# Two-level attention and a ReLU-squared layer: scores centred on the mean of h, softmax without transposes, four square blocks per 960 tokens

## The chip, the cores and the metric

One core of one Trainium2 chip runs the whole program. The metric is the device time in microseconds of one execution, the median of several. Engines: TensorE (PE in the profile, its weight loads PEld), VectorE (DVE), ScalarE (ACT), GpSimd (POOL); SyncE (SP) issues the DMAs.

## The reference

```python
x: [4, 12480, 128], inducing: [32, 128]; w_in: [128, 2048], w_out: [2048, 128]
def mab(q, kv):
    s = q @ kv.T / sqrt(128); a = softmax(s)       # over kv's rows
    return a @ kv
h = mab(inducing, x)            # per batch, 32 rows
y = mab(x, h)                   # per batch, 12480 rows
out = relu(y @ w_in) ** 2 @ w_out
```

Each row of y is a mean of 32 rows of h with weights a near 1/32. A hidden column keeps one sign for all tokens unless it is "mixed"; over the columns of positive sign the layer is a quadratic form in a, and both kernels compute it as such: products of differences a_i - a_j, squared, times 128-wide matrices made from w_in, h and w_out. Mixed columns are computed one by one.

## The kernel before, in words

x comes in twice: transposed (`xT`, fp32, tokens along the free axis) and in natural order (`xn`). A batch has 26 chunks of 480 tokens in 7 groups G of four (the last of two).

- `first(b)`: per group, scores of the inducing rows (line 226, four column groups of TensorE), evacuation with the scale and running maxima (245, `sT`); then the global maximum (260 to 271, `nb`), exp on ACT (286), four transposes (297, `et`) evacuated to `en`, products with `xn` (310, `hacc`) added up in `hq` (318). `largest` (277) takes abs-maxima of x on DVE, for a bound. At the end h and its transpose `hT` (327 to 333).
- `prepare(b)`: columns w_in against h (398, `hwv`), per-column signs (`pos`, `dead`, `mix`) from bounds, a linear part (482, `R`), a selection of up to 64 mixed columns (`hot`, 505 to 546), and four matrices of pair products (554, `G`; 558, `wq`) scaled into `w16` (559).
- `second(b, G)`: scores of x against h (226), evacuation (`s2`), transposes (350, `s2t`), token-major softmax (353 to 364: maximum, subtraction, exp, sum, reciprocal, product), transposes back (368, `at`), split into two fp16 halves (370, 371), stored to DRAM (`ad`, 372) and loaded again as `aT` with the 32 weights on each row quarter (382).
- `Chunk`: `up` multiplies `aT` by fixed difference matrices `pairs` (two tiles of two banks, each from two products on 64 rows, 591) and by `singles` (one bank of its own); `lift` squares the two wide tiles on ACT (603), and clips `singles` on DVE (607, `tmp`) and squares it on POOL (608); `down` sums a linear product (613, `lin`) and five products with `w16` (616) in one bank `po`, which ACT or DVE evacuates with scale and bias (620, 622), followed by the store of `o` (623).

Before the main loop come batch 0's `first`, the conversion of the weights from float64 words (`narrow`, 196 to 202), w_out's maximum (`prepare_w_out`, 208 to 213) and `prepare(0)`. In the main loop, chunk n's lifts, chunk n+1's ups and chunk n-1's downs are issued in turns, and `background(k)` hands out steps of `second` and of the next batch's `first` and `prepare` by fixed rates per chunk. Within what the buffers and data allow, a list scheduler with costs of its own orders each engine's queue; `to_act` chooses ACT or DVE for an evacuation by sums of estimated costs (`held`). A last part, entered only if a batch's flag says that the bounds fail (`flags`), computes all 2048 columns.

Of the kernel before, what the change touches and what calls it, by code (L numbers as in the profile page):

```python
# [9 lines left out]
F32 = mybir.dt.float32  # L10
# [27 lines left out]
def attend_then_relu2_mlp(ctx: ExitStack, tc: tile.TileContext, xn, xT, indT, w_in, w_out, outT):  # L38

# [20 lines left out]
    ps_s = ctx.enter_context(tc.tile_pool(name="ps_s", bufs=1, space=bass.MemoryType.PSUM))  # L60
# [14 lines left out]
    nc.vector.tensor_copy(rep, fold[:, 0:1].broadcast_to([P, 4, MI]))  # L75
    ones = const.tile([1, P], F32, name="ones")
# [15 lines left out]
    cut4 = const.tile([P, 1], F32, name="cut4")
    nc.vector.memset(cut4[0:64], 0.0)
    nc.vector.memset(cut4[64:P], -3e38)

    pairs = const.tile([P, 2 * P], F16, name="pairs")
    fold_f = fold.rearrange("p k i -> p (k i)")
    for s in range(1, 17):
        c, m = (s - 1) // 4, (s - 1) % 4
        rows = slice(64 * (c % 2), 64 * (c % 2) + 64)  # L100
        nc.vector.tensor_tensor(
            pairs[rows, P * (c // 2) + MI * m:P * (c // 2) + MI * (m + 1)], fold_f[rows, 0:MI], fold_f[rows, s:s + MI],
            op=ALU.subtract,
        )
# [4 lines left out]
    inv_t = const.tile([P, 1], F32, name="inv_t")  # L109
    flags = const.tile([1, NB], F32, name="flags")  # L110
# [5 lines left out]
    for k in range(2):  # L116
        one = Batch()
        one.xm = const.tile([P, NG], F32, name=f"xm{k}")
        one.hn = const.tile([P, P], F32, name=f"hn{k}")
        one.w16 = const.tile([P, NQ, P], F16, name=f"w16_{k}")  # L120
        one.lin = const.tile([P, P], F16, name=f"lin{k}")
        one.singles = const.tile([P, P], F16, name=f"singles{k}")
        nc.vector.memset(one.w16, 0.0)
        nc.vector.memset(one.singles, 0.0)
        nc.vector.tensor_copy(one.singles[0:64, 64:96], fold[0:64, 0])
        one.osc = const.tile([P, 1], F32, name=f"osc{k}")
        one.bias = const.tile([P, 1], F32, name=f"bias{k}")
# [21 lines left out]
    def evac(dst, src, cols, by=None):  # L149

        if to_act(120 + 0.833 * cols, 110 + 1.042 * cols):
# [19 lines left out]

# [34 lines left out]
    def prepare_w_out():  # L206
# [5 lines left out]
        nc.vector.reciprocal(t, inv_t)  # L212
        nc.scalar.mul(w_hi, wo_sb, t)
        yield


    def load_xT(b, G, again=False):
        pool, bufs = (mlp, 2) if again else (flow, NX)
        xp = pool.tile([P, 4, 4, TP], F32, tag="xp", name=f"xp_{b}_{G}_{again}", bufs=bufs)
        n = GRP[G]  # L220
        nc.sync.dma_start(xp[:, 0:n], xT[:, b, 16 * G:16 * G + 4 * n, :].rearrange("c (n q) p -> c n q p", q=4))
        return xp

    def scores(ps, lhsT, xp, n):
        for q in range(4):
            nc.tensor.matmul(  # L226
                ps[32 * q:32 * q + 32, 0:n * TP].rearrange("i (n p) -> i n p", p=TP),
                lhsT, xp[:, 0:n, q, :], start=True, stop=True,
            )

    def first(b):

        st = sts[b]
        sT = flow.tile([P, NCH * TP], F32, tag="sT", name=f"sT_{b}", bufs=1)
        mx = work.tile([P, NG], F32, tag="mx", name=f"mx_{b}")
        for G, n in enumerate(GRP):
            if b:
                st.xp[G] = load_xT(b, G)
                yield
            ps = att_psum(f"s1_{b}_{G}")  # L240
            xg = st.xp[G]
            scores(ps, indT_sb, xg, n)
            w = n * TP
            held["dve"] += 150 + 1.042 * w
            nc.vector.tensor_scalar(
                sT[:, 480 * G:480 * G + w], ps[:, 0:w], scale, None, op0=ALU.mult, op1=ALU.max, accum_out=mx[:, G:G + 1],
# [3 lines left out]
        def load_xn(h):  # L250

            if h >= NCH // 2:
                return None
            t = xnb[h % XB]
            nc.sync.dma_start(t, xn[b].rearrange("(p k) c -> p k c", p=TP)[:, 8 * h:8 * h + 8, :])
            return t

        xns = {h: load_xn(h) for h in range(XB)}
        m1 = small("m1")
        nc.vector.tensor_reduce(m1, mx, axis=AX.X, op=ALU.max)  # L260
# [13 lines left out]
        def largest(G):  # L274
            n = GRP[G]
            held["dve"] += 60 + 1.042 * 4 * n * TP
            nc.vector.tensor_reduce(  # L277
                st.xm[:, G:G + 1], st.xp[G][:, 0:n].rearrange("p n q t -> p (n q t)"), axis=AX.X, op=ALU.max,
                apply_absolute_value=True,
            )  # L280

        def exp(G):
            n = GRP[G]
            s = sT[:, 480 * G:480 * G + n * TP]
            held["act"] += 200 + 0.833 * n * TP
            nc.scalar.activation(s, s, AF.Exp, bias=nb, accum_out=zs[:, G:G + 1])  # L286

        zs = work.tile([P, NG], F32, tag="zs", name=f"zs_{b}")
        exp(0)
        exp(1)  # L290
        yield
        hq = work.tile([P, P + 1], F32, tag="hq", name=f"hq_{b}", bufs=1)
        for G, n in enumerate(GRP):
            ps = att_psum(f"et_{b}_{G}") if b else two_banks(f"et_{b}_{G}")[:, 0]
            for j in range(n):
                c = 4 * G + j
                nc.tensor.transpose(ps[0:TP, j * P:(j + 1) * P], sT[:, c * TP:(c + 1) * TP], ident)
            en = work.tile([TP, 4, P], F32, tag="en", name=f"en_{b}_{G}")
            evac(en[:, 0:n], ps[0:TP, 0:n * P].rearrange("p (n m) -> p n m", m=P), n * P)
            if G + 2 < NG:  # L300
                exp(G + 2)
            largest(G)
            yield
            hacc = att_psum(f"hacc_{b}_{G}")
            for h in range(n // 2):
                xg = xns.pop(2 * G + h)
                for j in (2 * h, 2 * h + 1):
                    c = 4 * G + j
                    for q in range(4):
                        st.last = nc.tensor.matmul(  # L310
                            hacc[32 * q:32 * q + 32, 0:P], en[:, j, 32 * q:32 * q + 32],
                            xg[:, 4 * (j % 2) + q, :], start=j == 0, stop=j == n - 1,
                        )
                xns[2 * G + h + XB] = load_xn(2 * G + h + XB)
# [4 lines left out]
            if G == NG - 1:  # L319
                nc.vector.tensor_reduce(hq[:, P:P + 1], zs, axis=AX.X, op=ALU.add)  # L320
            yield
        hs = att_psum(f"hs_{b}")
        nc.tensor.matmul(hs[:, 0:P + 1], rep.rearrange("p q i -> p (q i)"), hq, start=True, stop=True)
# [8 lines left out]
        nc.vector.tensor_reduce(st.hT[:, P:P + 1], ht[:, 0:MI], axis=AX.X, op=ALU.add)  # L332
        nc.vector.tensor_scalar(st.hT[:, P:P + 1], st.hT[:, P:P + 1], 1.0 / MI, None, op0=ALU.mult)
        yield

    def second(b, G, again=False):

        st = sts[b]
        n = GRP[G]
        t = 4 * n  # L340
        w = n * TP
        xp = st.xp.pop(G)
        ps = att_psum(f"s2_{b}_{G}")
        scores(ps, st.hT[:, 0:MI], xp, n)
        s2 = work.tile([P, 480], F32, tag="s2", name=f"s2s_{b}_{G}")
        evac(s2[:, 0:w], ps[:, 0:w], w)
        yield
        pt = att_psum(f"s2t_{b}_{G}")
        for j in range(n):
            nc.tensor.transpose(pt[0:TP, j * P:(j + 1) * P], s2[:, j * TP:(j + 1) * TP], ident)  # L350
        pv = pt[0:TP, 0:n * P].rearrange("p (t i) -> p t i", i=MI)
        mx = work.tile([TP, 16], F32, tag="mx2", name=f"mx2_{b}_{G}")
        nc.vector.tensor_reduce(mx[:, 0:t], pv, axis=AX.X, op=ALU.max)  # L353
        e = work.tile([TP, 16, MI], F32, tag="e2", name=f"e2_{b}_{G}")
# [536 lines left out]
```

## Time and profile before

| | |
|---|---|
| runs | 592.66 us median of 3 (591.72, 592.66, 596.0) |
| profiled execution | span 594.4 us, first to last instruction; it lies inside the range of the runs |
| busy: PE, PEld, DVE, ACT, POOL | 475.1, 229.3, 412.2, 326.5, 107.2 us |
| mean granted TensorE clock | 0.901 |
| DMA | 100.89 MB, 56.3% of 16 engines' time |
| first evacuation of an output tile | 132.11 us |
| last evacuation | 584.95 us |

A group's row reads: line, engine, operation, out<-in with shapes, count, busy time and mean ns of one, then the idle time just before it and what ended most of it. A row of the timeline starts with its start and its length in us; x8 stands for eight instructions in a row. An fp32 product is two records.

### The profile page before, as it was taken

What the parts mean: (1) busy time and instruction counts of PE and PEld (TensorE: products, weight loads), DVE (VectorE), ACT (ScalarE), POOL (GpSimd) and SP (SyncE); (2) the same over time, 40 slices, a digit from 0 to 9 for tenths busy, and PEclk for the clock granted to TensorE, in tenths of its full rate; (3) what the DMA queues carried; (4) which work ended last, traced back from release to release, by engine and by line L of the source; (5) the groups of instructions that cost most, each with busy time, mean ns of one, the idle gap of its engine ahead of it and who ended that gap; (6) DMA issues with size and microseconds to landing.
All of it is one profiled execution on the core that took longest, in us unless ns stands there. A gap on an engine that the chain in (4) does not pass through costs nothing. (4 is left out here: it accounts for less than half of the span.)

```text
span 594.4 us, 9822 instructions
## 1 busy us (share of the span) xinstructions
PE 475.1 (80%) x3539; PEld 229.3 (39%) x3539; DVE 412.2 (69%) x979; ACT 326.5 (55%) x475; POOL 107.2 (18%) x113
## 2 busy tenths in 40 slices
PE   4261373879899699988999799889998999899992
PEld 0140251643244265532344346433453455333330
DVE  6999519677774338877862578888844587888761
ACT  0040101247598346656698476475796565767770
POOL 0000000022031012112222111122211121233340
PEclk9775555899999759989999799999999899999998
DMA  8989473104669954346579863547588213254522
GB/s 343 327 212 243 160 193 115 52 1 156 211 191 239 267 149 145 109 157 220 145 211 259 247 189 117 183 133 215 167 223 224 79 51 101 83 178 139 167 108 79
DMA packets 52671, 100.89 MB, mean 170 GB/s; under 512 B 8476, under 2 KB 42268, under 8 KB 52604
## 3 DMA queue, kind: packets, MB, share of 16 engines
q1 hardware_dynamic: 52604, 100.08, 56.3%
q8 instruction: 32, 0.52, 0.4%
q14 instruction: 35, 0.29, 0.2%
HBM read 68.11 MB, written 31.95 MB: 168 GB/s over the span
## 5 line engine op out<-in xcount | busy, mean ns | idle before, releaser
L603 ACT ACTIVATE g<-hp 128x960 f16<-128x960 f32 x208 | 194.7, 976 | 43.3 <-PE hp L591 41.9
L608 POOL TENSOR_TENSOR g<-tmp 128x480 f16<-128x480 f32 x104 | 106.0, 1019 | 471.6 <-DVE tmp L607 271.0
L616 PE MATMUL po<-g,w 128*128 128x480 f16 x520 | 139.5, 378 | 0.4 <-ACT w L155 0.3
L607 DVE TENSOR_SCALAR tmp<-hs,off,cut 128x480 f32<-128x480 f32 x104 | 80.1, 770 | 28.8 <-PE hs L591 24.4
L591 PE MATMUL hp<-aT,pairs 64*128 64x480 f16 x416 | 87.6, 375 | 7.6 <-ACT g L603 7.5
L616 PEld LDWEIGHTS <-w 128*128 128x128 f16 x520 | 49.1, 99 | 71.1 <-issue 37.2
L620 ACT ACTIVATE o<-po,bias,osc 128x480 f32<-128x480 f32 x72 | 54.8, 761 | 33.8 <-PE po L616 28.5
L277 DVE TENSOR_REDUCE xm<-xp_False 128x1 f32<-128x1920 f32 (+1 forms) x28 | 56.0, 2002 | 7.0 <-DMA xp_False<-xT_dram 7.0
L613 PE MATMUL po<-aT,lin 128*128 128x480 f16 x104 | 39.8, 382 | 17.0 <-ACT o L620 12.0
L591 PEld LDWEIGHTS <-pairs 64*128 64x128 f16 x416 | 22.6, 93 | 75.0 <-issue 73.9
L310 PE MATMUL hacc<-xnb,en 120*32 120x128 f32 x832 | 36.0, 307 | 13.5 <-DMA xnb<-xn_dram 6.7
L591 PE MATMUL hs<-aT,singles 128*128 128x480 f16 x104 | 38.9, 374 | 2.6 <-DVE tmp L607 2.0
L226 PE MATMUL s<-xp_False,indT_sb 128*32 128x480 f32 (+1 forms) x224 | 29.8, 610 | 12.2 <-DMA xp_False<-xT_dram 8.3
L310 PEld LDWEIGHTS hacc<-xnb,en 120*32 120x32 f32 x832 | 23.3, 121 | 28.6 <-issue 9.8
L554 DVE TENSOR_TENSOR G<-hwp,hw 128x512 f16<-128x512 f16 x64 | 27.4, 459 | 8.1 <-PE wq L558 8.1
L286 ACT ACTIVATE sT<-sT,nb 128x480 f32<-128x480 f32 (+1 forms) x28 | 18.5, 665 | 26.5 <-DVE nb L271 26.5
L622 DVE TENSOR_SCALAR o<-po,osc,bias 128x480 f32<-128x480 f32 x32 | 24.8, 774 | 11.8 <-PE po L616 11.4
L226 PE MATMUL s<-xp_False,hT 128*32 128x480 f32 (+1 forms) x224 | 29.1, 593 | 1.2 <-DVE a L371 1.0
L359 ACT ACTIVATE e<-e 120x512 f32<-120x512 f32 (+1 forms) x28 | 16.9, 602 | 24.0 <-DVE e L355 23.7
L318 DVE TENSOR_TENSOR hq<-hacc,hq 128x128 f32<-128x128 f32 x24 | 6.9, 288 | 32.0 <-PE hacc L310 32.0
L153 ACT COPY en<-et 120x512 f32<-120x512 f32 (+1 forms) x26 | 14.4, 554 | 25.3 <-PE hacc L310 15.3
L353 DVE TENSOR_REDUCE mx<-s2t 120x16 f32<-120x512 f32 (+1 forms) x28 | 18.2, 649 | 10.5 <-PE s2t L350 9.9
(209 smaller groups left out, 586.9 us busy)
## 6 DMA issues: line engine op xcount, KB each, us to landing
xnb<-xn_dram SPq DMA_DIRECT2D x52, 480.0 KB, 6.4
outT_dram<-o SPq DMA_DIRECT2D x104, 240.0 KB, 2.5
xp_False<-xT_dram SPq DMA_DIRECT2D x24, 960.0 KB, 5.9
aT<-ad SPq DMA_DIRECT2D x96, 120.0 KB, 4.4
ad<-a SPq DMA_DIRECT2D x24, 240.0 KB, 2.4
wi<-w_in_dram SPq DMA_DIRECT2D x4, 512.0 KB, 15.7
wo<-w_out_dram SPq DMA_DIRECT2D x4, 512.0 KB, 7.0
xp_False<-xT_dram SPq DMA_DIRECT2D x4, 480.0 KB, 5.2
```

Source lines behind the costliest of these rows:

```text
L226: nc.tensor.matmul(ps[32 * q:32 * q + 32, 0:n * TP].rearrange("i (n p) -> i n p", p=TP), lhsT, xp[:, 0:n, q, :], start=True, stop=True,)
L277: nc.vector.tensor_reduce(st.xm[:, G:G + 1], st.xp[G][:, 0:n].rearrange("p n q t -> p (n q t)"), axis=AX.X, op=ALU.max, apply_absolute_val ...
L310: st.last = nc.tensor.matmul(hacc[32 * q:32 * q + 32, 0:P], en[:, j, 32 * q:32 * q + 32], xg[:, 4 * (j % 2) + q, :], start=j == 0, stop=j ...
L554: tt(g[:, :, MI * j:MI * j + MI], hwp, hw16f[:, :, s0:s0 + MI], op=ALU.mult)
L591: nc.tensor.matmul(hp[:, i, 0:CH].rearrange("p (q t) -> p q t", q=4), pairs[rows, j * P:(j + 1) * P] if j < 2 else st.singles, self.aT[row ...
L603: nc.scalar.activation(self.g[:, 2 * j:2 * j + 2], hp[:, 0:2, 0:CH], AF.Square)
L607: nc.vector.tensor_scalar(tmp, hp[:, 0, 0:CH], off4, cut4, op0=ALU.add, op1=ALU.max)
L608: nc.gpsimd.tensor_tensor(self.g[:, 4], tmp, tmp, op=ALU.mult)
L613: nc.tensor.matmul(po[:, 0:CH].rearrange("p (q t) -> p q t", q=4), st.lin, self.aT, start=True, stop=False)
L616: nc.tensor.matmul(po[:, 0:CH], st.w16[:, i], self.g[:, i], start=False, stop=i == NQ - 1)
L620: nc.scalar.activation(o, po[:, 0:CH], AF.Identity, bias=st.bias, scale=st.osc)
L622: nc.vector.tensor_scalar(o, po[:, 0:CH], st.osc, st.bias, op0=ALU.mult, op1=ALU.add)
```

## The change

- Scores of x against h become scores against h minus its mean (`dhT`), computed in `prepare` for all groups with their abs-maximum (`bm`), which gives both the bound (`largest` goes) and a common shift `nb2`. A group tile holds four chunks of 480 tokens, one per 32-row quarter, in every step.
- `second` is exp, one fp32 product with `sums` (blocks of -1/1024) that gives each token's sum on all its rows, one DVE operation that turns it into normalised weights, and one that writes the centred weights in fp16 (`d16`). No transposes, no DRAM round trip. The reciprocal is replaced by its first-order form.
- In `first`, the transposes become one 32x32 block transpose on DVE; `hacc` has 15 products.
- `Duo` replaces `Chunk`: two chunks, 32 rows each. Four up tiles of two banks (`pairs` 0 to 2, and `pair3` with up to 16 mixed columns in its last 16 columns), three squared on ACT, the fourth clipped on DVE and squared on POOL; `po` has two banks; `lin` is fp32 on 32 rows. `singles` and the fifth weight matrix go.
- Layouts: a group of `xT` is 7.5 KB contiguous per partition, `xn` has 15 tokens per partition, one load per group. Buffers: 7 of `xT`, 3 of `xn` (before 9 and 4 half-sized).
- Order: w_in's loads between x's, w_out's before the last parts of `xn`; `narrow` starts during the first scores; x loads of the next batch have steps of their own; rates of `background` per duo.

```diff
     def second(b, G):
+        e = st.s2[G]
+        nc.scalar.activation(e[0:r], e[0:r], AF.Exp, bias=st.nb2[0:r])
+        nc.tensor.matmul(ps[0:r, 0:CH], sums[0:r, 0:r], e[0:r], start=True, stop=True)
+        yield
+        nc.vector.scalar_tensor_tensor(e[0:r], ps[0:r, 0:CH], (2.0 - 1e-9 / MI) / MI, e[0:r], op0=ALU.add, op1=ALU.mult)
+        nc.vector.tensor_scalar(d[0:r], e[0:r], -1.0 / MI, S_D, op0=ALU.add, op1=ALU.mult)
...
     def prepare(b):
+        for G, n in enumerate(GRP):
+            scores(ps, st.dhT[:, 0:MI], st.xp.pop(G), n)
+            evac(st.s2[G][0:r], ps[0:r, 0:CH], CH, scale)
+            nc.vector.tensor_reduce(
+                st.bm[0:r, G:G + 1], st.s2[G][0:r], axis=AX.X, op=ALU.max, apply_absolute_value=True,
+            )
+            if G in (2, 4):
+                columns(G // 2 - 1)
+            yield
...
     def first(b):
+            nc.vector.transpose(en[0:r].rearrange("p k i -> p (k i)"), sT[G][0:r])
...
+            for k in range(NBLK):
+                c = 32 * (k % 4)
+                st.last = nc.tensor.matmul(
+                    hacc[c:c + 32, 0:P], en[0:r, k, :], xg[0:r, k, :], start=k < 4, stop=k >= NBLK - 4,
+                )
...
+    class Duo:
         def up(self, j):
+            for i in range(2):
+                r = self.rows(i)
+                nc.tensor.matmul(hp[:, i, 0:CH], w[r], st.d16[self.G][r], start=True, stop=True)
         def lift(self, j):
+            if j < NC - 1:
+                nc.scalar.activation(self.g[:, j], hp[:, :, 0:CH], AF.Square)
+                return
+            nc.vector.tensor_scalar(tmp, hp[:, :, 0:CH], st.off, cut, op0=ALU.add, op1=ALU.max)
+            nc.gpsimd.tensor_tensor(self.g[:, j], tmp, tmp, op=ALU.mult)
         def down(self):
+            po = ps_o.tile([P, 2, 512], F32, tag="po", name=f"po_{self.b}_{self.d}")
+            for i in range(2):
+                r = self.rows(i)
+                nc.tensor.matmul(po[:, i, 0:CH], st.lin[r], st.s2[self.G][r], start=True, stop=False)
+            yield
+            for n, j in enumerate((3, 0, 1, 2)):
+                for i in range(2):
+                    nc.tensor.matmul(po[:, i, 0:CH], st.w16[:, j], self.g[:, j, i], start=False, stop=n == NC - 1)
+                yield
...
+    for k, (n, j) in enumerate(steps):
+        duo = duos[n]
+        if j == 3:
+            drain(dn)
+            dn = duos[n - 1].down() if n else iter(())
+        duo.lift(j)
+        up(k + 2)
+        next(dn, None)
+        if j in (0, 1):
+            next(dn, None)
+        background(duo.b, duo.d + (k % 4 + 1) / 4)
```

More of the change, by code (lines that the diff above doesn't have):

```diff
@@ L132, in attend_then_relu2_mlp @@
         st.hT = const.tile([P, P + 1], F32, name=f"hT{b}")
-        st.xp, st.aT = {}, {}
-    xnb = [const.tile([TP, 8, P], F32, name=f"xnb{i}") for i in range(XB)]
+        st.xp, st.xn, st.s2, st.d16 = {}, {}, {}, {}
     flow_pools, start_pools = ExitStack(), ExitStack()
@@ L231, in first, with loads, score_tile @@
+    def loads(b):
+        st = sts[b]
+        for G in range(NG):
+            st.xp[G] = load_xT(b, G)
+            yield
+        for G in range(XB):
+            st.xn[G] = load_xn(b, G)
+            yield
+    def scores(ps, lhsT, xp, n):
+        for q in range(n):
+            nc.tensor.matmul(ps[32 * q:32 * q + 32, 0:CH], lhsT, xp[:, q, :], start=True, stop=True)
+    def score_tile(name):
+        return flow.tile([P, CH], F32, tag="s", name=name, bufs=14)
     def first(b):
         st = sts[b]
-        sT = flow.tile([P, NCH * TP], F32, tag="sT", name=f"sT_{b}", bufs=1)
@@ L258, in first @@
-        xns = {h: load_xn(h) for h in range(XB)}
         m1 = small("m1")
-        nc.vector.tensor_reduce(m1, mx, axis=AX.X, op=ALU.max)
+        nc.vector.tensor_reduce(m1, st.mx, axis=AX.X, op=ALU.max)
         tp = att_psum(f"mt_{b}")
@@ L272, in first @@
         yield
[L274 to L280, printed above, removed]
-        def exp(G):
[L283 to L288, printed above, removed]
+        def exp(G):
+            r = 32 * GRP[G]
+            held["act"] += 420 + 0.833 * CH
+            nc.scalar.activation(sT[G][0:r], sT[G][0:r], AF.Exp, bias=nb[0:r], accum_out=st.zs[0:r, G:G + 1])
         exp(0)
-        exp(1)
         yield
@@ L293, in first @@
         for G, n in enumerate(GRP):
[L294 to L302, printed above, removed]
+            r = 32 * n
+            en = work.tile([P, NBLK, MI], F32, tag="en", name=f"en_{b}_{G}")
+            held["dve"] += 100 + 1.042 * CH
+            nc.vector.transpose(en[0:r].rearrange("p k i -> p (k i)"), sT[G][0:r])
+            if G + 1 < NG:
+                exp(G + 1)
             yield
             hacc = att_psum(f"hacc_{b}_{G}")
[L305 to L314, printed above, removed]
+            xg = st.xn.pop(G)
+            for k in range(NBLK):
[3 more added lines that the diff above has]
+                )
+            if G + XB < NG:
+                st.xn[G + XB] = load_xn(b, G + XB)
+            held["dve"] += 288
             if G == 0:
@@ L420, in prepare @@
+        ts(am4[:, 2:3], am4[:, 2:3], 2.0 ** -20, None, op0=ALU.mult)
+        nc.vector.tensor_reduce(am2[:, 0:1], am4, axis=AX.X, op=ALU.max)
+        nc.vector.tensor_reduce(am2[:, 1:2], st.bm, axis=AX.X, op=ALU.max)
         yield
         ps = att_psum(f"am_{b}")
-        nc.tensor.transpose(ps[0:1, 0:P], am, ident)
-        nc.tensor.matmul(ps[0:1, P:P + MI], xm, dh, start=True, stop=True)
+        for k in range(2):
+            nc.tensor.transpose(ps[0:1, k * P:k * P + P], am2[:, k:k + 1], ident)
@@ L513, in prepare @@
[L513 to L523 removed]
+        ps = att_psum(f"R_{b}")
@@ new lines, in prepare @@
+        for k in range(NF):
+            nc.tensor.matmul(ps[0:MI + 1, 0:P], hwS[:, k], wo_sb[:, k], start=k == 0, stop=k == NF - 1)
+        cat = work.tile([MI + 1, P], F32, tag="cat", name=f"cat_{b}")
+        nc.vector.tensor_copy(cat, ps[0:MI + 1, 0:P])
+        yield
+        ps = att_psum(f"kv_{b}")
+        for k in range(NF):
+            nc.tensor.matmul(ps[96:P, 0:MI + 1], hot[:, k], hws[:, k], start=k == 0, stop=k == NF - 1)
+        kv = work.tile([P, 4, MI], F32, tag="kv", name=f"kv_{b}")
@@ L546, in prepare @@
-        ts(st.w16[0:MX, 4], ps[0:MX, 0:P], tsg[0:MX, 4:5], None, op0=ALU.mult)
-        nc.vector.memset(wm[:, 4:5], 0.0)
-        nc.vector.tensor_reduce(wm[0:MX, 4:5], ps[0:MX, 0:P], axis=AX.X, op=ALU.max, apply_absolute_value=True)
-        yield
-        for c in range(4):
-            g = flow.tile([P, NF, P], F16, tag="G", name=f"G_{b}_{c}")
+        nc.tensor.matmul(ps[:, 0:P], rep1, cat, start=True, stop=True)
+        ts(st.lin, ps[:, 0:P], t18, None, op0=ALU.mult)
+        bs = att_psum(f"bs_{b}")
@@ L661, in attend_then_relu2_mlp @@
     mlp_pools = ExitStack()
-    mlp = mlp_pools.enter_context(tc.tile_pool(name="mlp", bufs=3, reuse_waits="tile"))
-    N_SECOND, N_SCORES, N_HEADS, N_PRE = 4, 2 * NG, 20, 26
-    ahead = chain(*(second(b, G) for b in range(NB) for G in range(NG)))
-    nexts = {b: chain(first(b), prepare(b)) for b in range(1, NB)}
-    given = {"ahead": 0, **{b: 0 for b in nexts}}
-    def give(what, gen, want):
+    mlp = mlp_pools.enter_context(tc.tile_pool(name="mlp", bufs=2, reuse_waits="tile"))
+    N_LOADS, N_SCORES, N_HEADS, N_PRE, N_SECOND = NG + XB, NG, 2 + 1 + 2 * NG + 2, 7 + 18, 2
@@ L670, in give @@
+    gens = {"a": chain(*(second(b, G) for b in range(NB) for G in range(NG)))}
+    for b in range(1, NB):
+        gens["x", b] = loads(b)
+        gens["h", b] = chain(first(b), prepare(b))
+    given = dict.fromkeys(gens, 0)
+    def give(what, want):
         while given[what] < want:
-            next(gen, None)
+            next(gens[what], None)
             given[what] += 1
     for n, _ in enumerate(prepare(0)):
-        give("ahead", ahead, min(n + 1, 2 * N_SECOND))
-    with tc.issue_after(sts[0].last.ins):
-        give(1, nexts[1], 4)
@@ new lines, in attend_then_relu2_mlp, with up @@
+    duos = [Duo(b, d) for b in range(NB) for d in range(NCH // 2)]
+    steps = [(n, j) for n in range(len(duos)) for j in (3, 0, 1, 2)]
+    def up(k):
+        if k < len(steps):
+            n, j = steps[k]
+            if j == 3 and duos[n].d == 0 and duos[n].b:
+                drain(gens["h", duos[n].b])
+            duos[n].up(j)
+    up(0)
+    up(1)
+    dn = iter(())
+    for k, (n, j) in enumerate(steps):
[9 more added lines that the diff above has]
+        background(duo.b, duo.d + (k % 4 + 1) / 4)
```

527 lines of the change are left out of this document (238 added, 289 removed).

## The prediction

> **What bounds the kernel now.** I read the page's shares first, then a table by stages, cut where the first output tile is evacuated (132 us), where the last quadratic weight of a batch is reduced (260, 387, 507) and at the end of the last evacuation.
>
> ```profile
> span 594.4 us, 9822 instructions
> PE 475.1 (80%) x3539; PEld 229.3 (39%) x3539; DVE 412.2 (69%) x979; ACT 326.5 (55%) x475; POOL 107.2 (18%) x113
> PEclk9775555899999759989999799999999899999998
> ...
> 132.00:260.00 128.00, 114.05 (x858) 55.51 (x856) 83.11 (x204) 80.94 (x121) 23.83 (x23) 0.92 0.63 183
> 260.00:387.00 127.00, 113.56 (x884) 53.40 (x884) 88.62 (x211) 85.75 (x127) 26.16 (x26) 0.96 0.65 190
> 387.00:507.00 120.00, 111.33 (x879) 53.41 (x880) 85.20 (x214) 80.37 (x118) 26.55 (x26) 0.99 0.50 148
> 507.00:586.00 79.00, 70.17 (x370) 26.41 (x368) 60.13 (x102) 55.18 (x67) 26.46 (x26) 1.00 0.42 137
> ```
>
> Columns of a stage: length, busy time of PE, weight loads, DVE, ACT and POOL, granted clock, DMA share, GB/s. TensorE is busy 409 of 454 us from 132 on (114.05 + 113.56 + 111.33 + 70.17), 90%; DVE has 70%, ACT 67%. So after the front only what leaves TensorE's queue pays; DVE and ACT work pays where TensorE waits for it, at most the other 45 us. The front is another case: the clock digits are 5 there.
>
> Busy spans of matmuls overlap, so I price them from start to next start, at full clock:
>
> ```profile
> 545.30 1.17 PE L616 MATMUL po<-g,w 128*128 128x480 f16 x5
> 546.40 0.38 PE L591 MATMUL hp<-aT,pairs 64*128 64x480 f16 x2
> 546.71 0.38 PE L591 MATMUL hs<-aT,singles 128*128 128x480 f16 x1
> 546.96 0.63 PE L368 MATMUL at<-ident,e 120*128 120x120 f32 x4
> 547.51 0.61 PE L226 MATMUL s<-xp_False,hT 128*32 128x240 f32 x8
> 548.06 0.38 PE L591 MATMUL hp<-aT,pairs 64*128 64x480 f16 x2
> 548.37 0.38 PE L613 MATMUL po<-aT,lin 128*128 128x480 f16 x1
> 548.58 1.18 PE L616 MATMUL po<-g,w 128*128 128x480 f16 x5
> ...
> 132.58 1.01 PE L226 MATMUL s<-xp_False,indT_sb 128*32 128x480 f32 x8
> 133.53 0.38 PE L613 MATMUL po<-aT,lin 128*128 128x480 f16 x1
> ...
> 303.82 1.08 PE L310 MATMUL hacc<-xnb,en 120*32 120x128 f32 x32
> 304.83 0.65 PE L297 MATMUL et<-ident,sT 128*120 128x128 f32 x4
> 305.32 0.37 PE L613 MATMUL po<-aT,lin 128*128 128x480 f16 x1
> ```
>
> Five po cost 1.10 (545.30 to 546.40), so 0.22 each. A pair of hp on two halves of the rows costs 0.31 together (546.40 to 546.71): the two run at once. hs costs 0.25, lin 0.21. One chunk is 1.10 + 2 x 0.31 + 0.25 + 0.21 = 2.18, two chunks 4.36. A score group (four column groups, fp32) costs 0.95, four transposes at 0.55, et 0.49; s2t, of et's form, I put at 0.5; hacc 1.01 per group.
>
> **The change, part by part.**
>
> *Main loop, TensorE.* A duo (two chunks) issues four up pairs on 32 rows; the nearest row is hp on 64 rows, 0.31: 1.24. Eight w16 matmuls at 0.22: 1.76. Two lin matmuls become fp32 on 32 rows. No row shows fp32 row groups. From below: the pair runs at once, like the four column groups of a score: 0.95. From above: one after the other, each two fp32 passes of 0.40: 1.75. I take 0.95, since all groups in the rows above, of columns in fp32 and of rows in fp16, run at once. Sum 3.95 against 4.36: 0.41 less, 5.3 us in 13 duos.
>
> *Attention, TensorE.* Per group of four chunks et, s2t and at go (0.49 + 0.5 + 0.55 = 1.54); the product with `sums` comes, fp32, full array, two passes of 480 columns like one score group: 0.95, from 0.85 to 1.9 if its passes are dearer. hacc has 15 instead of 16 products, 0.06 less. Net 0.65 less, in 6.5 full groups 4.2 us. The two score products stay, but the second set moves from its own batch into the preparation before it.
>
> *Preparation, TensorE.* The 16 products of line 545 go (their share of the selected columns joins the fourth block), the others keep number and shape or shrink: 1 to 1.5 us less.
>
> A full batch loses 5.3 + 4.2 + 1.3 = 10.8 us of PE work at full clock. At the 0.92 to 0.99 clock and 90% occupancy of the stages that is 12.5 us each, 37.5 for three. The last batch loses 5.3 and about six score groups, 5.7, that ran inside it: 11.
>
> *DVE and ACT.*
>
> ```profile
> L603 ACT ACTIVATE g<-hp 128x960 f16<-128x960 f32 x208 | 194.7, 976 | 43.3 <-PE hp L591 41.9
> L607 DVE TENSOR_SCALAR tmp<-hs,off,cut 128x480 f32<-128x480 f32 x104 | 80.1, 770 | 28.8 <-PE hs L591 24.4
> L277 DVE TENSOR_REDUCE xm<-xp_False 128x1 f32<-128x1920 f32 (+1 forms) x28 | 56.0, 2002 | 7.0 <-DMA xp_False<-xT_dram 7.0
> L353 DVE TENSOR_REDUCE mx<-s2t 120x16 f32<-120x512 f32 (+1 forms) x28 | 18.2, 649 | 10.5 <-PE s2t L350 9.9
> L364 DVE TENSOR_TENSOR e<-e,z 120x512 f32<-120x512 f32 x24 | 19.3, 803 | 0.4
> L450 DVE CAST hw<-hws 128x512 f16<-128x512 f32 x4 | 1.7, 422 | 0.0
> ```
>
> Squares fall from 208 to 156: 52 x 0.976 = 51 us off ACT. DVE loses `largest` (56.0) and the token-major softmax: six operations per group, four of the size of L353's or L364's row, some 3.6 us x 28 = 100. It gains per group an abs-max, a product with the reciprocal and a 32x32 transpose at 0.65 (L353's size) and a narrowing at 0.42 (L450): 2.4 x 28 = 66. tmp becomes 52 of 128x960; L607 gives 0.77 for 480 columns, so 1.2 to 1.5 each, the same 62 to 78 us. DVE falls to about 320, ACT to 250 or less. I cost this at nothing, hidden behind TensorE; without that cover the 45 us of waits are what it could move, either way. The transpose has no row: from 0.42 (a plain copy) to 1.6 (twice the dearest row), 28 times, off the path except in the front.
>
> [...]
>
> *Waits and queues.* The second softmax's exp now waits for `nb2`, so for the abs-max of all seven groups of its batch; behind it on ACT stand the squares, and behind those the up products. It is issued from duo 12 of the batch before, after the preparation's 25 steps are due, so I cost it at nothing; if the preparation is late the boundary stalls by that lateness, three times. The 28 stores and 112 reloads of the attention weights (`ad`, `aT`) leave SP's queue. POOL squares the same columns in half as many instructions, and its product is needed a duo later: nothing. The x loads move ahead of stores they followed:
>
> ```profile
> SPq L372 <- DVE a L371: 72.3, 21, 7.7
> SPq L255 <- PE hacc L310: 49.8, 22, 17.2
> ```
>
> A natural-order load that waits for hacc still holds the stores behind it, 17.2 us at most here; three o buffers now hold 3 duos, some 25 us: nothing.
>
> *Front.*
>
> ```profile
> 28.28 0.16 DVE L271 TENSOR_SCALAR nb<-mb 128x1 f32<-128x1 f32 x1 [0.40 <-PE mb L269]
> 62.57 2.15 DVE L277 TENSOR_REDUCE xm<-xp_False 128x1 f32<-128x1920 f32 x1 [2.79 <-DMA xp_False<-xT_dram]
> 68.32 0.37 PE L173 MATMUL wo_t<-ident,wmax 128*1 128x128 f32 x1 [15.91 <-DVE wmax L208]
> 75.34 0.65 PE L310 MATMUL hacc<-xnb,en 120*32 120x128 f32 x16 [1.89 <-DMA xnb<-xn_dram]
> 78.29 0.29 DVE L331 COPY hT<-ht 128x128 f32<-128x128 f32 x1 [0.63 <-PE ht L330]
> 132.11 0.75 ACT L620 ACTIVATE o<-po,bias,osc 128x480 f32<-128x480 f32 x1 [0.67 <-PE po L616]
> ...
> 0.00:30.00 30.00, 11.35 (x62) 2.78 (x63) 24.82 (x69) 2.75 (x5) 1.22 (x9) 0.87 0.94 334
> 75.00:90.00 15.00, 11.39 (x63) 8.69 (x63) 3.80 (x14) 1.32 (x3) 0.00 (x0) 0.57 0.68 181
> ```
>
> PE waits 15.91 us for w_out's maximum with the rest of hacc queued behind it; DVE in turn waits at 62.57 with a `largest` for the next batch's x. Both orders go: narrowing starts among the first scores, w_out is loaded before the last three x parts. What is late next is DMA: 12.8 MB of x and 4.2 MB of weights at 334 GB/s are 51 us, then the last hacc and 3 us to hT (75.34 to 78.29): hT at 58 to 62 instead of 78. From hT to the first output are 54 us now; five more score groups at half clock (twice 0.95 each) come in, two softmax groups and line 545 go: I take 56. First output at 116, 16 us earlier; from 8 to 26.
>
> **Sum**: 594.4 - 16 - 37.5 - 11 = 530 for the profiled span. That span lies 1.7 us above the runs' median of 592.66 (591.72 to 596.0), so 528 as a median.
>
> **The rivals.** *The lin pair runs one after the other*: 0.8 x 52 = 42 us more: 570. For it: fp32 row groups are shown nowhere.
>
> *Evacuation becomes the bound.* hs had a bank of its own; now four tiles share two buffers, and po, two banks wide, is single: tmp (1.3) and o (1.3) in DVE's one queue, then four ups (1.24), lin (0.95) and eight products (1.76) in PE's make a ring of 6.6 us, 6.7 with hand-overs. In full batches a duo has over 8 us and this hides; in the last it lasts 87 instead of 68, and a few us at each boundary: 555. For it: fewer buffers for as many evacuations. Against it: in the rows of L603 and L607 ACT and DVE wait for PE (41.9 and 24.4 us).
>
> *The clock halves: slower.* TensorE's share drops, and where it drops far enough the clock goes: 76% busy at 0.57 in the row of 75 to 90, 88% and more at 0.92 to 1.00 in the stages. The place is the main loop, where waits of the preparation open. Of about 370 us of PE work after 116, each us run at half clock adds one; from 64 us on, a sixth, the change loses; a quarter gives 530 + 92 = 622. Against it: fp16 streams still fill every duo.
>
> [...]
>
> *All comes better*: 95% occupancy and a front of 106: 502.
>
> *It falls back.* Limits got tighter (16 mixed columns instead of 64), and a failed flag runs the full-width path. Computed from the reference's inputs, at most 1 column is mixed, rho is 0.00028 at most against 0.0039: practically excluded; 104 chunks of 64 products at 0.22 would come on top, some 1,460 us.
>
> **How the numbers follow.** Forecast 0.60, lin in series 0.13, evacuation 0.11, better 0.07, clock 0.08, fallback 0.01. The range 500 to 572 takes in all but the tails of these. A measurement of this kernel tells 1% from nothing: faster 0.89, same 0.03, slower 0.08.
>
> **What would show it.** Right: the hT copy near 60, the first o near 116, batches of some 115, 115 and 108, a last one of 68; PE still near 90%; lin pairs within 1.0 us. Wrong: lin pairs of 1.7; long PE gaps for tmp or o; clock digits of 5 beyond the front; a batch's first duo waiting for exp.

## The result and the profile after

The changed kernel takes 517.89 us (514.31 to 518.57) against 592.66: 0.8709 of it, with a 95% interval from 0.866 to 0.8758. Forecast were 528 us. The profile shown here is of a second run of the same kernel, `a0_again` below, since the one recorded with the result fell into a disturbed execution of 618 us.

Its page, the span, the shares and the clock:

```profile
span 514.4 us, 7934 instructions
PE 422.4 (82%) x3083; PEld 182.4 (35%) x3083; DVE 311.2 (60%) x754; ACT 239.8 (47%) x326; POOL 95.7 (19%) x62
PEclk9555676769999998999799789999898989998995
```

The stages, cut at the first evacuation of an output, at the last reduction of quadratic weights of batches 1 to 3, and at the last evacuation; the last row is the whole loop:

```profile
119.80:214.40 94.60, 86.58 (x704) 40.80 (x703) 55.61 (x138) 57.89 (x80) 20.10 (x11) 0.95 0.53 194
214.40:324.70 110.30, 102.99 (x771) 44.09 (x770) 67.01 (x160) 60.31 (x83) 23.70 (x13) 0.92 0.47 175
324.70:433.90 109.20, 100.49 (x771) 43.51 (x771) 68.43 (x160) 60.46 (x83) 23.69 (x13) 0.94 0.25 91
433.90:503.60 69.70, 62.74 (x281) 19.29 (x280) 38.49 (x46) 36.74 (x40) 23.24 (x13) 0.96 0.25 101
119.80:503.60 383.80, 352.80 (x2524) 147.69 (x2522) 229.54 (x500) 215.40 (x283) 90.73 (x50) 0.94 0.38 142
```

The same stretch of the kernel before, from its first to its last evacuation:

```profile
132.10:584.90 452.80, 409.03 (x2989) 188.73 (x2988) 316.19 (x726) 302.25 (x432) 103.00 (x101) 0.96 0.56 168
```

From here on this stretch, from the first to the last evacuation of an output, is called the loop. Of the 80 us of span, 69.0 went from the loop and 12.3 from the front (the first evacuation came at 132.1). A run's time is some 1.8 us above its span (516.27 for 514.4), so the profile before shows an execution of about 596 us, at the upper end of its runs, and the spans lie 80 us apart where the medians lie 75. In the loop TensorE was busy 56.2 us less and waited 12.8 less (43.8 before, 31.0 after). It is 92% busy now, while its clock fell from 0.96 to 0.94.

The timeline after: h's copy, the first output, and a duo of the last batch, from lin to the next lin.

```profile
64.61 0.29 DVE L332 COPY hT<-ht 128x128 f32<-128x128 f32 x1 [0.48 <-PE ht L331]
119.78 1.15 ACT L572 ACTIVATE o<-po,bias,osc 128x960 f32<-128x960 f32 x1 [1.45 <-PE po L568]
...
480.85 1.07 PE L564 MATMUL po<-s,lin 32*128 32x480 f32 x4
481.86 0.98 PE L568 MATMUL po<-g,w 128*128 128x480 f16 x4
482.77 0.38 PE L543 MATMUL hp<-d,pair 32*128 32x480 f16 x2
483.08 0.98 PE L568 MATMUL po<-g,w 128*128 128x480 f16 x4
484.00 0.37 PE L543 MATMUL hp<-d,pairs 32*128 32x480 f16 x2
484.59 0.38 PE L543 MATMUL hp<-d,pairs 32*128 32x480 f16 x2 [0.22 <-DVE tmp L556]
485.51 0.38 PE L543 MATMUL hp<-d,pairs 32*128 32x480 f16 x2 [0.55 <-ACT g L552]
485.78 1.07 PE L564 MATMUL po<-s,lin 32*128 32x480 f32 x4
```

Here one reads the two rivals that hung on the duo. The two lin products, four records, take 1.01 us from start to next start (480.85 to 481.86): they run at once. This duo takes 4.93 us (480.85 to 485.78), with two waits of 0.22 and 0.55, and the 13 duos of the last stage 69.7 us: no ring of 6.7, and not the 87 us of that rival.

The groups whose durations had been guessed:

```profile
L552 ACT ACTIVATE g<-hp 128x960 f16<-128x960 f32 x156 | 146.2, 968 | 103.5 <-PE hp L543 103.3
L556 DVE TENSOR_SCALAR tmp<-hp,off,cut 128x960 f32<-128x960 f32 x52 | 66.2, 1273 | 44.8 <-PE hp L543 44.6
L347 ACT ACTIVATE s<-s,nb 128x480 f32<-128x480 f32 x24 | 15.2, 686 | 3.9 <-DVE k L419 3.9
L302 DVE STREAM_TRANSPOSE en<-sT 128x480 f32<-128x480 f32 x24 | 15.6, 663 | 0.0
```

### The profile page after: what moved, and what is told of

It reads as the page before. It is cut to its first block, busy times and chain, and to the rows that moved or that the text cites. A ratio compares the mean times of both kernels' runs of the same rounds, so it can differ in the third digit from the quotient of the medians.

```text
span 616.4 us, 7934 instructions
## 1 busy us (share of the span) xinstructions
PE 543.1 (88%) x3083; PEld 208.0 (34%) x3083; DVE 309.4 (50%) x754; ACT 243.1 (39%) x326; POOL 95.8 (16%) x62
## 4 chain that ended last, share of the span: by engine, by line
PE 82%; DVE 9%; DMA 3%; ACT 2%; issue 2%; SPq 1%; ACTq 0%
PE po L568 23%; PE s L255 12%; PE po L564 10%; PE hp L543 10%; PE hacc L310 7%; PE z L349 6%; PE hwv L371 4%; PE R L469 4%; PE wq L508 4%; DMA xp_False<-xT_dram 3%; ACT g L552 2%; PE kv L475 1%; DVE G L502 1%; DVE gm L282 1%; DVE no_r L211 0%
## 5 line engine op out<-in xcount | busy, mean ns | idle before, releaser
L552 ACT ACTIVATE g<-hp 128x960 f16<-128x960 f32 x156 | 148.2, 968 | 144.3 <-PE hp L543 143.0
L557 POOL TENSOR_TENSOR g<-tmp 128x960 f16<-128x960 f32 x52 | 94.6, 1818 | 499.5 <-DVE tmp L556 285.5
L556 DVE TENSOR_SCALAR tmp<-hp,off,cut 128x960 f32<-128x960 f32 x52 | 66.2, 1274 | 67.7 <-PE hp L543 67.6
L564 PE MATMUL po<-s,lin 32*128 32x480 f32 x208 | 91.4, 847 | 2.7 <-DVE o L574 1.4
L543 PE MATMUL hp<-d,pairs 32*128 32x480 f16 x312 | 67.5, 447 | 10.2 <-ACT g L552 8.8
L572 ACT ACTIVATE o<-po,bias,osc 128x960 f32<-128x960 f32 x28 | 32.2, 1150 | 56.3 <-PE po L568 56.2
L255 PE MATMUL s<-xp_False,indT_sb 128*32 128x480 f32 x208 | 41.4, 826 | 12.3 <-DMA xp_False<-xT_dram 9.3
L310 PE MATMUL hacc<-xn,en 128*32 128x128 f32 (+1 forms) x840 | 45.2, 365 | 5.4 <-issue 3.3
L255 PE MATMUL s<-xp_False,dhT 128*32 128x480 f32 x208 | 44.0, 910 | 1.2 <-DVE dhT L337 1.2
L349 PE MATMUL z<-s,sums 128*128 128x480 f32 (+1 forms) x56 | 40.9, 825 | 1.6 <-ACT s L347 1.6
L168 ACT ACTIVATE s<-s 128x480 f32<-128x480 f32 (+1 forms) x28 | 15.9, 569 | 38.6 <-PE s L255 38.6
```

What stands on the lines that cost most here:

```text
L255: nc.tensor.matmul(ps[32 * q:32 * q + 32, 0:CH], lhsT, xp[:, q, :], start=True, stop=True)
L310: st.last = nc.tensor.matmul(hacc[c:c + 32, 0:P], en[0:r, k, :], xg[0:r, k, :], start=k < 4, stop=k >= NBLK - 4,)
L349: nc.tensor.matmul(ps[0:r, 0:CH], sums[0:r, 0:r], e[0:r], start=True, stop=True)
L543: nc.tensor.matmul(hp[:, i, 0:CH], w[r], st.d16[self.G][r], start=True, stop=True)
L552: nc.scalar.activation(self.g[:, j], hp[:, :, 0:CH], AF.Square)
L556: nc.vector.tensor_scalar(tmp, hp[:, :, 0:CH], st.off, cut, op0=ALU.add, op1=ALU.max)
```

## The experiments

All ratios are to the kernel before, timed on the same chip. The rows come from three chips, on which the kernel before had medians of 590.43 to 594.88 us, so a difference of a few us between rows is better read from the ratios. "After" is the changed kernel. The code cuts show the lines that matter; `...` stands for what is left out.

| run | us | ratio [95%] |
|---|---|---|
| `a0_again`: after, again | 516.25 | 0.8723 [0.8667, 0.878] |
| `e1_lin16`: lin in fp16 | 483.18 | 0.8153 [0.8096, 0.8211] |
| `e2_largest`: after, maxima put back | 535.63 | 0.9047 [0.8986, 0.9108] |
| `b1_no_largest`: before, without maxima | 577.2 | 0.9716 [0.9634, 0.9799] |
| `e3_old_front` | 517.9 | 0.8733 [0.8675, 0.879] |
| `e4_sums_twice` | 528.8 | 0.8852 [0.8785, 0.8919] |
| `e5_act_extra` | 512.81 | 0.8646 [0.8608, 0.8684] |
| `e8_pieces` | 544.07 | 0.9173 [0.9112, 0.9234] |
| `e6_lin16_front` | 480.77 | 0.8107 [0.8052, 0.8162] |
| `e7_one_burst` | 472.07 | 0.7957 [0.7917, 0.7996] |
| `e9_fill_before_r` | 471.25 | 0.7936 [0.7903, 0.7969] |
| `e10_fill_after_kv` | 480.31 | 0.811 [0.8074, 0.8145] |

**The kernel again.**

> The changed kernel once more, for a profile beside the following ones. Theory (TensorE's queue sets the time after the front): 518 us within 1%; PE busy near 90% of the span behind the front, waits of PE for tmp, o or g under 30 us in all; the two lin products of a duo start within 0.02 us of each other. Rival (evacuation sets it): PE under 80% busy behind the front, and its longest waits are for o and tmp.

It gave the profile above.

**lin in fp16.** `lin` multiplies the centred weights `d16` on the same 32 rows, with the scales adapted.

```diff
-        one.lin = const.tile([P, P], F32, name=f"lin{k}")
+        one.lin = const.tile([P, P], F16, name=f"lin{k}")
...
-                nc.tensor.matmul(po[:, i, 0:CH], st.lin[r], st.s2[self.G][r], start=True, stop=False)
+                nc.tensor.matmul(po[:, i, 0:CH], st.lin[r], st.d16[self.G][r], start=True, stop=False)
```

> lin as one fp16 pass on the centred fp16 weights d16 instead of fp32 on the fp32 weights; w16 and the output scale are shifted by 2**6 to fit. A duo's lin pair drops from 0.95 us to about 0.31 of TensorE's time. Theory (TensorE's queue sets the time): 52 x 0.64 = 33 us less, some 485 us, a bit more where clock is below full. Rival (evacuation and DVE's queue set it): under 8 us less.

The loop of this run:

```profile
115.50:469.60 354.10, 314.69 (x2422) 133.80 (x2422) 231.42 (x500) 213.76 (x283) 91.43 (x50) 0.94 0.42 154
```

33 us less, as the theory had it. TensorE is busy 38.1 us less in the loop (352.80 to 314.69) and waits 8.4 more, so the loop is 29.7 shorter (383.8 to 354.1). What leaves the duos' own queue pays for the most part.

**The maxima, put back and taken out.** In after, 28 abs-maxima of 128x1920 on VectorE whose result nobody reads; in before, `largest` left out (the bound uses a constant 0.5, so before computes other limits).

```diff
...
+            nc.vector.tensor_reduce(st.xm[:, G:G + 1], st.xp[G][:, 0:n].rearrange("p n t -> p (n t)"), axis=AX.X,
+                op=ALU.max, apply_absolute_value=True)
```

> The changed kernel with the 28 abs-maxima of x on DVE put back where the old kernel had them (2.0 us each, 56 us of DVE; the result is used nowhere). Theory (TensorE's queue sets the time; DVE's relief by itself is worth little): 2 to 10 us more, most of it in the front, where DVE narrows the weights. Rival (a good part of the gain is DVE's relief): 25 to 50 us more.

> The old kernel without its 28 abs-maxima of x on DVE (a constant 0.5 stands in the bound, which still holds; the output formula is the same). 56 us of DVE go. Theory (TensorE's queue sets the time): the front gets 5 to 12 us shorter, since w_out's maximum no longer stands behind waits for the next batch's x, and the rest 0 to 10 us: 575 to 588 us. Rival (DVE's relief is a good part of the gain): 540 to 565 us.

Put back they cost 19 us, between theory and rival; taken out of before they gave 13, inside the range. The loops, first of after with maxima, then of before without:

```profile
127.00:522.80 395.80, 361.40 (x2524) 146.92 (x2522) 252.07 (x515) 215.87 (x283) 90.77 (x50) 0.93 0.38 138
```

```profile
125.50:560.80 435.30, 401.74 (x2989) 183.96 (x2988) 311.36 (x743) 282.55 (x397) 102.48 (x101) 0.98 0.59 175
```

And the copy of h in before without maxima, which stood at 78.29 with them:

```profile
69.63 0.29 DVE L331 COPY hT<-ht 128x128 f32<-128x128 f32 x1 [0.63 <-PE ht L330]
```

After with maxima has its first evacuation 7.2 us later than in `a0_again` (11.4 to 11.9 later than in three other profiles with the same front, see `e3_old_front`) and a loop 12.0 longer. In that loop TensorE's waits grew by 3.4 (31.0 to 34.4), but the same 2524 records were busy 8.6 us longer; with those at half clock counted by half, 3.7 of it are left, so 4.9 are the clock. Less than a third of the loop's price is TensorE waiting; why the records took 3.7 us more at full clock is open. In before it was both: waits fall by 10.2 (43.8 to 33.6), busy time by 7.3 for the same 2989 records, and the clock rises from 0.96 to 0.98.

The price is not spread evenly. In after, 14 of the 28 maxima run ahead of the first output and seven each within the first two batches of the loop. Taken from a batch's first output to the next batch's, these two are 7.7 and 5.4 us longer, the last two 1.2 longer and 2.2 shorter. In before, 15.0 of the 17.5 us by which the loop got shorter lie in the first batch (135.6 to 120.6), though maxima run in the next two as well. And that pair of profiles is 24 us apart where the medians are 13, so part of the 15.0 may be the longer run that the profile of before shows.

**The maxima in pieces.**

```diff
...
+            for q in range(n):
+                nc.vector.tensor_reduce(st.xm[:, 4 * G + q:4 * G + q + 1], st.xp[G][:, q], axis=AX.X,
+                    op=ALU.max, apply_absolute_value=True)
```

> The changed kernel with the 28 abs-maxima put back in four pieces of 480 columns each (104 of about 0.65 us, 68 us of VectorE instead of 56), against 535.6 us with whole ones of 2 us and 516 without. Theory (a 2 us instruction stands whole ahead of tmp, o or a step of the preparation's chain, so that the length of a piece decides): 518 to 527, the batches after the front at most 2 us longer than without. Rival (the sum of VectorE's work decides): 536 to 545, each batch 3 to 6 us longer than without.

```profile
127.20:526.70 399.50, 363.77 (x2524) 148.54 (x2524) 262.36 (x559) 215.65 (x283) 90.69 (x50) 0.91 0.37 137
```

The median is 544 us and all four runs lie at 538.34 or more, so the theory is out: the length of one instruction is not what counts. The time is in the rival's range. Whether pieces are dearer than whole maxima is not told: 56 us of maxima cost 19, 68 us in pieces cost 22 by the profiled executions (538.34 against 516.27) and 28 by the medians. Not each batch got longer, as the rival had it: the first two of the loop by 6.9 and 8.9 us, the others by 1.0 and -1.0, and the maxima lie in those two again. The loop is 15.7 longer than without them, and 11.0 of it is busy time of the same 2524 records (352.80 to 363.77), at a clock of 0.91.

**ScalarE.**

```diff
+                if j == 2:
...
+                    nc.scalar.activation(x, self.g[:, j], AF.Square)
```

> ScalarE squares one 128x960 tile of each duo once more into a tile that nobody reads, 52 more instructions of about 1 us, some 50 us of ScalarE and nothing on TensorE. Theory (an engine at 47% busy has room for it, less dear than VectorE's maxima, which cost a third of their length): 0 to 8 us more, 516 to 524. First rival (it costs a third of its length as the maxima did): 13 to 20 us more, 529 to 536. Second rival (the squares stand in a serial chain with the up products): over 25 us more, beyond 541.

```profile
115.10:495.80 380.70, 349.49 (x2524) 145.16 (x2522) 230.62 (x501) 264.56 (x333) 90.73 (x50) 0.95 0.38 143
```

512.81 us, 3 less than after, and the intervals of the ratios overlap: 50 us of ScalarE cost nothing. VectorE's price is not a price of every engine off the path. But the place differs too: the extra squares stand in the duos, the maxima in `first`. Extra VectorE work within the duos was not tried.

**The product with ones, twice.**

```diff
+        nc.tensor.matmul(ps[0:r, 0:CH], sums[0:r, 0:r], e[0:r], start=True, stop=True)
```

> The product with ones (z) is issued twice into the same bank, 28 more fp32 products of about 1.0 us, 28 us of TensorE in all. Theory (TensorE's queue sets the time, a microsecond of its work costs a microsecond): 24 to 28 us more, 540 to 544, about 7 in each full batch. Rival (the softmax's products lie in waits that exist anyway, so that only the elementwise work counts): 0 to 6 us more, at most 522.

```profile
115.60:516.20 400.60, 379.97 (x2574) 155.08 (x2572) 229.13 (x501) 216.33 (x283) 90.25 (x50) 0.92 0.37 136
```

Neither: 12.6 us by the medians (7.6 by the ratios). In the loop TensorE is busy 27.2 us more and waits 10.4 less (31.0 to 20.6), so the loop is 16.8 longer (383.8 to 400.6) and more than a third of the work fell into waits that existed. The times differ by less than the loops because the first evacuation came at 115.6 here and at 119.8 in `a0_again`; more on that spread below.

**The old order in front.**

```diff
...
     def weights():
         for j in range(4):
             narrow(w_in_sb[:, 512 * j:512 * j + 512], words["wi", j], f"ni{j}")
             yield
+        for j in range(4):
+            words["wo", j] = load_words(w_out[512 * j:512 * j + 512, :].rearrange("(f p) d -> p f d", p=P), f"wo{j}")
+        yield
...
-        if n % 2:
+        if n >= NG + 1:
             next(wgen, None)
```

> Only the order in front of the first batch is put back: w_in's transfers behind all of xT, w_out's behind w_in's conversions, a step of conversion only once the scores are given. Compared with the changed kernel's 516 us. Theory (the prediction's 16 us in front are the order's): first output at 127 to 133 instead of 116.7, 526 to 532 us. Rival (the cheaper chain from h to the first group made the front shorter, not the order): first output below 121, at most 520 us. The lengths of the later batches stay within 1 us of 110 by either.

```profile
68.56 0.29 DVE L332 COPY hT<-ht 128x128 f32<-128x128 f32 x1 [0.63 <-PE ht L331]
```

The rival's numbers held: 517.9 us, and the first evacuation at 118.6, not at 127 to 133. h came at 68.6, against 64.6, 64.9, 65.2 and 65.3 in four profiles with the new order (`a0_again`, `e1_lin16`, `e4_sums_twice`, `e5_act_extra`). Their first evacuations lie at 119.8, 115.5, 115.6 and 115.1, so 118.6 is within their spread. The new order gave h some 4 us, and nothing that shows in the time. The rival's cause held only in part: from h to the first evacuation took 50.0 us here and 53.8 in before, while h itself came 9.7 us earlier than there, under the old order.

**w_out behind h.** On the fp16 lin.

```diff
     for n, _ in enumerate(first(0)):
-        if n % 2:
+        if n % 2 and n < 8:
             next(wgen, None)
-    drain(wgen)
...
     for n, _ in enumerate(prepare(0)):
+        next(wgen, None)
...
+    drain(wgen)
```

> The kernel with lin in fp16 (483 us) with one more edit: w_out's conversion and maximum are given in step with the preparation of batch 0 behind h, instead of between the exponentials and h's products, where 18.5 us of VectorE work and the maximum's transpose in TensorE's queue hold h up. Theory: hT at 52 to 57 instead of 65, the conversions fall into VectorE's waits behind it, first output 4 to 9 us earlier than 109, 474 to 479 us. Rival (VectorE's sum of work in front sets it wherever it stands): first output within 2 us of 109, 481 to 485.

```profile
58.16 0.29 DVE L332 COPY hT<-ht 128x128 f32<-128x128 f32 x1 [0.63 <-PE ht L331]
```

h came 6.7 us earlier than in `e1_lin16` (64.9) and the first evacuation at 109.5 instead of 115.5, but the loop was 3.2 us longer. The times, 480.77 and 483.18, are not told apart: unclear as a whole, shown for the front (109.4 to 111.4 in all four kernels that have it).

**One burst.** On top of it, the eight w16 products of a duo one after the other.

```diff
-        next(dn, None)
-        if j in (0, 1):
+        if j != 0:
             next(dn, None)
+        if j == 1:
+            for _ in range(3):
+                next(dn, None)
```

> The kernel of e6 (481 us) with the eight w16 products of a duo issued in one burst, instead of two bursts of four with an up pair between. The traces show a w16 product at 0.202 us when another follows, 0.298 when a product on a row quarter follows. Theory (a change of row grouping costs 0.1 us of TensorE, and one burst saves two of them a duo): 0.2 x 52 = 10 us less work, 470 to 475 us. Rival (the later products hold po and the evacuation back, and the waits for it take back what the changes gave): 479 us or more, with more idle time of TensorE ahead of the up and lin products.

```profile
111.40:455.80 344.40, 301.23 (x2422) 134.28 (x2422) 229.42 (x500) 212.87 (x283) 91.88 (x50) 0.96 0.43 158
```

472.07 us, inside the theory's range. Its reason holds by half. Taken at full clock, TensorE's work in the loop fell by 6.8 us, of which lin and the up pairs, that now stand side by side, gave 7.1; changes from a w16 product to another kind fell from 120 to 95 only, in the whole run. The rest of the 14.2 us of busy time came from the clock (0.93 to 0.96).

**Idle time filled.** Ten fp16 products of 128x512 whose result nobody reads, ahead of `pl`, or behind `kv`. In the preparation, `pl` is a small product just ahead of R, `kv` one that follows R. The edit for the first place:

```diff
+        warm = att_psum(f"warm_{b}")
+        for _ in range(10):
+            nc.tensor.matmul(warm, pairs[:, 0:P], hwp.rearrange("p k i -> p (k i)"), start=True, stop=True)
         bp = att_psum(f"pl_{b}")
```

> The kernel of e7 (472 us) with ten fp16 products per batch, 2.1 us of TensorE, whose result nobody reads, behind hwp and ahead of pl: where the queue stands still for VectorE's chain (about 2 of 3.4 us), just before R, whose 32 records then run at half clock (0.21 apart). Theory (a stretch of 3.4 us with little work halves the clock of the next one): R at full clock in most batches, 0.11 apart, 2 to 4 us less per later batch at the price of nothing or half a microsecond, 463 to 470 us: more work, less time. Rival (the clock follows something else, and the products count): R as before, 472 to 480.

> The same ten products per batch, but behind kv and ahead of kq, where TensorE has work and the clock is full again. By the theory of e9 they count in full, 8.5 us in four batches: 478 to 482, R still 0.21 apart. By the rival of e9 (only the sum of the work counts) this and e9 come out alike, within 3 us.

R of the batches 1 and 2 in the kernel of `e7_one_burst`:

```profile
180.52 0.39 PE L455 MATMUL pl<-inc,before 128*128 128x1 f32 x2 [1.68 <-DVE inc L450]
180.96 5.23 PE L469 MATMUL R<-wo_sb,hwS 128*33 128x128 f32 x32
...
281.14 0.59 PE L455 MATMUL pl<-inc,before 128*128 128x1 f32 x2 [1.86 <-DVE inc L450]
281.78 6.00 PE L469 MATMUL R<-wo_sb,hwS 128*33 128x128 f32 x32
```

And with the products ahead of `pl`:

```profile
178.41 0.38 PE L458 MATMUL pl<-inc,before 128*128 128x1 f32 x2 [1.48 <-DVE inc L450]
178.84 5.35 PE L472 MATMUL R<-wo_sb,hwS 128*33 128x128 f32 x32
...
279.30 2.33 PE L456 MATMUL warm<-hwp,pairs 128*128 128x512 f16 x10
281.46 0.28 PE L458 MATMUL pl<-inc,before 128*128 128x1 f32 x2
282.10 3.68 PE L472 MATMUL R<-wo_sb,hwS 128*33 128x128 f32 x32
```

Where the filler came directly ahead of R (279.30) the wait is gone and R takes 3.68 us instead of 6.00. Where it came early (batch 1, and batch 3 likewise) a wait of 1.48 stayed, and R stayed slow. So of the three later batches it worked in one, not in most. The sum is nothing: 471.25 against 472.07, short of the theory's 463 to 470. But the same work behind `kv` cost 8.2 us (480.31), as expected there. So 8.5 us of TensorE work cost 8 in one place and nothing in another; the rival, by which only the sum counts, is refuted. What paid for it ahead of `pl` is both a wait that was filled and a clock that was kept: the loop's waits fall by 2.4 us (43.2 to 40.8), and what is lost to half clock by 3.6 (13.8 to 10.2). Behind `kv` the waits grow by 2.1 and the loss by 1.5.

## Why the prediction was right, point by point

To compare with its terms I took TensorE's records of the loop from start to next start, without the waits, and counted those at half clock by half (in before a w16 product ahead of another takes 0.203 us at full clock and 0.400 at half, a record of R 0.110 and 0.212):

| us of TensorE at full clock, first to last evacuation | before | after | gone | forecast |
|---|---|---|---|---|
| chunks and duos (up, w16, lin) | 244.0 | 198.3 | 45.7 | 21 |
| attention (scores, transposes, `sums`, hacc) | 97.9 | 82.0 | 15.9 | 18 |
| preparation and rest | 51.5 | 47.8 | 3.7 | 4 |
| lost to half clock | 15.3 | 21.8 | -6.5 | 5, waits included |
| waits | 43.8 | 31.0 | 12.8 | |

The rows add up to 452.5 and 380.9 of the loops' 452.8 and 383.8 us.

- **Main loop.** The step that failed is "one chunk is 2.18, two chunks 4.36". The duo came out as priced (198.3 / 51 = 3.9, forecast 3.95). The chunk before was dearer, 4.8 for two: over the loop hs takes 0.31 in the mean instead of 0.25, a pair of hp 0.36 instead of 0.31, as some stand alone, and five w16 1.15 instead of 1.10. I had taken each from one place in the last batch. hs, from the loop before:

```profile
390.08 0.38 PE L591 MATMUL hs<-aT,singles 128*128 128x480 f16 x1
390.39 0.58 PE L591 MATMUL hp<-aT,pairs 64*128 64x480 f16 x4
```

  An up pair follows it there, 0.31 later; at 546.71 a transpose had followed after 0.25. With the means the forecast would have been some 25 us lower.
- **lin** at once: 1.01 in the duo above and 0.92 in the mean of the loop, against 0.95. **Attention** and **preparation** by their terms.
- **Front.** 16 forecast; 12.3 found in this profile, 16.5 to 17.0 in the three others with the same order in front. From h to the first output 56 forecast, 55.2 found here and 49.8 to 50.6 in those three, where TensorE was busy 38.7 to 40.0 us in that stretch instead of 44.0. So the hit of 55.2 is in part luck. h came at 64.6 instead of 58 to 62, because w_out's maximum still stands ahead of hacc's products; `e6_lin16_front`, which moves it, has 58.2. The prediction let two things go, a `largest` in VectorE's queue and the order of loads and conversions, and did not price them apart. At h, which moved by 13.7 us (78.3 to 64.6), the first is the larger: taking `largest` alone out of before gives 8.7 (69.6, `b1_no_largest`), undoing the order alone in after takes back 4.0 (68.6, `e3_old_front`).
- **VectorE and ScalarE at nothing.** Their sums were right (311 and 240 us for "about 320" and "250 or less"), the price wrong for VectorE: all in all a microsecond of it was worth 0.24 (13 of 56, `b1_no_largest`), 0.34 (19 of 56, `e2_largest`) and 0.32 to 0.41 (`e8_pieces`), with most of it in the front and the first two batches. ScalarE's was nothing. The bound of 45 us held for the waits, which moved by 12.8.
- **The transpose.** 0.663 us for 0.65. Abs-maxima of 480 columns, as many as it has, take 0.637 us (`e8_pieces`), of 960 and 1920 columns 1.144 and 2.145 us (line 277 of before), so some 1.04 ns a column and 0.14 us besides.
- **The new wait** for `nb2` cost little or nothing: ScalarE's idle time ahead of that exp is 3.9 us over four batches.
- **The clock.** The rival's mechanism is there but small: 6.5 us more than before, in these two executions. The mean granted clock of the four runs of `a0_again` goes from 0.871, in this profile, to 0.895, so a few us of such a row are chance.
- **The sum.** Span 514.4 instead of 530: 25 us too little for the duo and 8 for the waits (12.8 against the 5), too much by 6.5 for the clock, 4 for the front, 2 for the attention, and 4 behind the last evacuation and in what the table doesn't add up. The direction and the rank of the parts held, the two largest errors were terms too small. That the total came within 16 us is in part luck: 33 us of terms too small stand against some 17 too large. Batch by batch, from first output to first output, 135.6, 125.7, 120.3 and 71.2 us became 106.4, 110.9, 106.5 and 59.9. The duos took 9 to 13 off each batch, for 5.3 forecast; in the later three, more half clock took a good part of that back, and in the first, waits and half clock fell by 6 us each.

## What to carry to other kernels

A product's price in a mixed queue depends on what follows it (0.25 or 0.31 us for hs, 0.205 or 0.29 for w16): take it as a mean over the loop, from start to next start, not from one clean row. VectorE at 60% wasn't free here: a microsecond more of it cost a quarter to two fifths, and where it cost, TensorE waited more and had a lower clock (in `e2_largest` 34.4 us for 31.0, and 0.93 for 0.94). ScalarE at 47% took 50 us more for nothing, though in another place of the program. And before a front is credited to a new order, undo the order alone, and compare several profiles: the same front varied by almost 5 us.

## What the runs showed of the hardware

**The clock follows stretches of 3.41 us, and what is in them.** In the profiles of before and after, each period of one granted clock lasts a whole multiple of 3.41 us, the last alone excepted. Two stretches of after, each with the one behind it:

```profile
187.50:190.90 3.40, 1.09 (x6) 0.32 (x5) 3.40 (x13) 3.40 (x6) 0.00 (x0) 1.00 0.65 251
190.90:197.70 6.80, 6.67 (x31) 5.20 (x31) 4.45 (x14) 3.54 (x6) 2.24 (x1) 0.50 0.44 147
...
283.10:286.50 3.40, 3.40 (x27) 2.27 (x28) 2.26 (x4) 1.92 (x3) 0.71 (x1) 1.00 0.95 314
286.50:293.30 6.80, 6.80 (x24) 1.36 (x17) 3.35 (x15) 2.95 (x4) 0.00 (x0) 0.50 0.84 350
```

The first was busy 1.09 of 3.40 us, and the clock behind it was 0.50. The second was busy throughout, but with products of 33 columns (hwv) and on few rows, and half clock followed too. Over the loops of thirteen profiles, before and the twelve runs of the table, 50 of 63 stretches at full clock with 1.4 us or more of waiting were followed by half clock, and 17 of 941 with less than 0.5; 14 of these 17 held hwv's products, the other three mostly products on 32 or 64 rows. Of the 13 that kept the clock in spite of the waiting, 11 held mostly products on all 128 rows and columns (po or wq). What in these products goes with the clock, their rows, their columns or something else, was not isolated.

**Ahead of another split of the array, a w16 product took 0.09 us more.** In the timeline of the last batch four w16 products take 0.91 us up to a product on 32 rows (481.86 to 482.77). Over the loop of after, at full clock and where nothing waits, a w16 product takes 0.205 us ahead of another w16 (305 of them) and 0.203 ahead of other products on all 128 rows that are not split into column groups (15), but 0.292 to 0.298 ahead of products on 32 rows or in groups of 32 columns (77). In before it takes 0.203 ahead of another w16, and 0.298 ahead of products on 64 rows. So what goes with the 0.09 us is another split of the array, not another kind of product. What fills them was not isolated.
